# Residual block on one core: the last chunk's outer weight combinations in three operations of 1024 columns

## The chip, the cores and the metric

The kernel runs on one core of a Trainium2 chip. The metric is device time in microseconds (us), and less is better. Several runs are timed, and one further kind of record, the profile, shows a single execution instruction by instruction. The engines are named as in the profile: PE is TensorE (matrix products), DVE is VectorE, ACT is ScalarE, POOL is GpSimd, SP is SyncE, which only issues DMAs here.

## The reference

The kernel computes a residual block with a time embedding, as in diffusion models, over two images of 512 channels and 64 x 64 pixels:

```python
def gn(z, gamma, beta):              # 4 groups of 128 channels
    zr = z.reshape(B, G, (C // G) * H * W)
    mu = zr.mean(-1).reshape(B, G, 1)
    var = ((zr - mu) ** 2).mean(-1).reshape(B, G, 1)
    zn = ((zr - mu) / jnp.sqrt(var + eps)).reshape(B, C, H, W)
    return zn * gamma.reshape(1, C, 1, 1) + beta.reshape(1, C, 1, 1)
...
h = conv3(_silu(gn(x, g1, be1)), w1)      # 3x3, padding 1, 512 -> 512
emb = _silu(t_emb) @ w_emb
h = h + emb.reshape(B, C, 1, 1)
h = conv3(_silu(gn(h, g2, be2)), w2)
return x + h
```

Inputs and weights are bf16. Nearly all of the arithmetic lies in the two 3 x 3 convolutions.

## The kernel before

**Tiling.** Channels are cut into four blocks of 128 (`ct` for input, `k` for output blocks). The image is cut into two halves of 32 rows, and a convolution over one half of one image is a *chunk*. There are eight: 0 to 3 are the first convolution, 4 to 7 the second. A *unit* is one output block of one chunk, so each chunk has four units, 32 in all; the code names the unit of chunk 6 and output block 3 `u63`. Every value that is worked on lies in one large 16-bit tile in SBUF, `ar`, whose regions are given by offsets, and products land in the eight banks of `psum`.

**The convolution as a transform.** The rows of a half are transformed in groups of four, so that a 3 x 3 convolution over the rows takes six products of transformed rows (numbered 0 to 5) in place of more direct ones. 0 to 3 are the inner ones, 4 and 5 the outer ones. Along a row, a second, smaller transform ("nested") is used: the pixels are split into even and odd ones, and a product with three taps becomes four products with combined weights of 256 columns instead of three of 512. In chunks 4 to 6 the inner products are nested and the outer ones are plain; in the last chunk, 7, the outer ones are nested too. Nested products need weight combinations: of three taps w0, w1, w2 one forms w0 + w2, then (w0 + w2) + w1 and (w0 + w2) - w1.

**The last chunk.** `unit7` (line 890) is the unit of chunk 7. It calls `nest_st` (line 882), which forms the combinations of the outer weights of that unit. These weights are streamed from memory for each unit by `stream_w2` (line 664) in two loads, one for two input blocks each, into one of two sets of SBUF space (`s` is 0 or 1, by turns; `st_off` gives the place). `nest_st` forms the sums for two input blocks in three additions of 512 columns, then for the other two. The difference is written over the middle tap, in place. `B_mms`, `A_mms`, `Bo_mms` and `Ao_mms` list the matmuls of the nested products: `B` and `A` are the inner ones, `Bo` and `Ao` the outer ones. The steps of a unit are, in this order: four inner `B` steps, four inner `A` steps, two `Bo` steps and two `Ao` steps, each with eight matmuls of 256 columns. ACT copies the results from `psum` into `ar` with a scale (names `b`, `m`, `o4`, `o5`). Pairs of banks are used in turn, so a step of a unit waits until the pair's earlier result has been copied. DVE then adds: `S` (sum and difference of the nested halves), `A` (the halves added together), `s` and `d` (sum and difference of the product pairs), then the scalings by 8, 2 and 4 on the engines that `CFG["s"]` names for the chunk, `y` (the inner product sums into the result rows `ys`) and two `O` additions, which add the outer products `OS` and `OA`. A DMA on POOL's queue adds the finished unit to the output in memory, where the block's input x has been copied before. The result rows have two buffers, `YS[0]` and `YS[1]`, by turns.

The very last unit ends in `last_y` (line 1110), which works in smaller pieces and stores with three plain DMAs on SP's queue.

**What sets the order.** The kernel writes no engine's order by hand. `Plan.op` records every operation with the space it reads and writes, and an assumed cost; `Plan._run` is a list scheduler over these, which takes on each engine the ready operation of the best priority; `Plan.solve` makes the priorities in three rounds, changes them by the tables `NUDGE` and `ORDER`, and fixes the order; `Plan.emit` then writes the instructions in this order. PE's products form one chain, so their order is the order of the program. A plain DMA is paced: `emit` adds a wait for a matmul that the plan has shortly before the DMA's own place. Where an instruction stands in its engine's queue is so an outcome of the plan; on the chip the engines run in order, and wait for each other by semaphores.

All DVE additions have line 423 in the profile, all DVE scalings line 427, all ACT operations line 446, all DMAs line 459, nearly all matmuls line 474.

Of the kernel before, what the change touches and what calls it, by code (L numbers as in the profile page):

```python
# [10 lines left out]
ACT = mybir.ActivationFunctionType  # L11
ALU = mybir.AluOpType
# [9 lines left out]
class Op:  # L22
# [3 lines left out]
NUDGE = {  # L26
    ('a10', 'DMA'): -6.1,
    ('emb', 'DMA'): -4.9,
    ('k01', 'DVE'): 3.6,
    ('k10', 'DVE'): -17.9,  # L30
    ('ld_ur02', 'DMA'): -31,
    ('ld_ur11', 'DMA'): -12.6,
    ('ld_ur12', 'DMA'): 4.6,
    ('ld_ur13', 'DMA'): -26.7,
    ('ld_ur21', 'DMA'): -3.1,
    ('ld_ur23', 'DMA'): -69.1,
    ('ld_ur3', 'DMA'): -62.2,
    ('rob10', 'DVE'): -6,
    ('row11', 'DVE'): 19.2,
    ('silu00', 'ACT'): -8.7,  # L40
    ('silu11', 'ACT'): -0.4,
    ('st01', 'DVE'): 24.1,
    ('st02', 'ACT'): 36.2,
    ('st02', 'PE'): 26.8,
    ('st03', 'ACT'): 61.3,
    ('st10', 'ACT'): -3.4,
    ('st11', 'ACT'): -24.7,
    ('u004', 'DVE'): 81.3,
    ('u00d', 'DVE'): -4.5,
    ('u00y', 'DVE'): -1.5,  # L50
    ('u01m1', 'ACT'): -14.6,
    ('w1_00', 'DMA'): 12.8,
    ('w1_01', 'DMA'): -14.6,
    ('w1_03', 'ACT'): 45.4,
    ('w1_13', 'DVE'): 35.8,
    ('w1_20', 'DVE'): 27.3,
    ('w1_22', 'ACT'): 48.7,
    ('w1_22', 'DVE'): 67.4,
    ('w1_23', 'DVE'): 187.4,
    ('w1_31', 'ACT'): 16.7,  # L60
    ('w1_33', 'ACT'): 79.1,
}


ORDER = (2, (
    (204379228, 255, 30, 1),
    (234843898, 319, 120, 1),
    (211139775, 268, 30, 3),
    (669684967, 433, 15, 3),
    (1006773657, 341, 15, 3),  # L70
    (788794351, 91, 15, 3),
    (40166790, 349, 60, 1),
    (920935792, 232, 15, 1),
    (410399867, 107, 60, 0.3),
    (420875362, 192, 15, 1),
    (385567171, 251, 30, 3),
    (279912161, 95, 30, 0.3),
    (315890846, 329, 120, 1),
    (696499368, 218, 60, 1),
    (272137600, 194, 15, 0.3),  # L80
    (605732795, 129, 30, 1),
    (29479506, 139, 15, 1),
    (973994246, 204, 15, 1),
    (488781037, 250, 30, 1),
    (34394231, 99, 30, 0.3),
    (655024064, 49, 30, 0.3),
    (144588941, 58, 60, 0.3),
    (252865214, 352, 15, 1),
    (1046031975, 342, 30, 1),
    (242005847, 138, 15, 1),  # L90
    (974414065, 143, 15, 1),
    (73604465, 212, 30, 3),
    (659385421, 129, 15, 1),
    (738286652, 264, 120, 3),
    (573361134, 368, 15, 1),
))


class Plan:
# [118 lines left out]
    def solve(self, rounds=3):  # L218
        ops = self.ops
# [5 lines left out]
        pris, best = [], None  # L225
        for k in range(rounds):
            pris.append(pri)
            st, span = self._run(pri, False)
            if k + 1 == rounds:
                break  # L230
            bt, bspan = self._run([-(s + o.cost) for s, o in zip(st, ops)], True)
            pri = [-(b + o.cost) for b, o in zip(bt, ops)]
        k, moves = ORDER
        pri = np.array(pris[k]) - np.array([NUDGE.get((o.name, o.eng), 0.0) for o in ops])
        st = np.array(self._run(pri.tolist(), False)[0])
        for seed, t0, w, sg in moves:
            pri = pri + np.where((st >= t0) & (st < t0 + w), np.random.default_rng(seed).normal(size=n) * sg, 0.0)
        best = self._run(pri.tolist(), False)
        self.span = best[1]
        for o, s in zip(ops, best[0]):  # L240
            o.start = s
        return best

    PACE = 0.8
# [1202 lines left out]
```

## Time and profile before

| | us |
|---|---|
| median of 4 runs | 459.6 |
| the runs | 456.84, 458.66, 460.55, 462.36 |
| the profiled execution, its own time | 462.36 |
| its span, from first to last instruction | 460.4 |
| busy: PE, DVE, ACT, POOL | 444.6, 432.7, 391.9, 66.6 |

The profile's lines are read as follows. A group line has the source line, the engine, the operation, what it writes and reads, shapes and count; then the busy time in us and the mean of one in ns; then how long the engine stood idle just before such instructions and what ended most of that idle time. A timeline line has start, duration, engine and operation, a count of merged instructions, and in brackets the idle time before them and who ended it. A line of the stretches has for each engine the busy time and, in brackets, the number of instructions. A matmul's own duration is longer than its distance to the next one, since matmuls are pipelined.

### The profile page before, as it was taken

What the parts mean: (1) busy time and instruction counts of PE and PEld (TensorE: products, weight loads), DVE (VectorE), ACT (ScalarE), POOL (GpSimd) and SP (SyncE); (2) the same over time, 40 slices, a digit from 0 to 9 for tenths busy, and PEclk for the clock granted to TensorE, in tenths of its full rate; (3) what the DMA queues carried; (4) which work ended last, traced back from release to release, by engine and by line L of the source; (5) the groups of instructions that cost most, each with busy time, mean ns of one, the idle gap of its engine ahead of it and who ended that gap; (6) DMA issues with size and microseconds to landing.
All of it is one profiled execution on the core that took longest, in us unless ns stands there. A gap on an engine that the chain in (4) does not pass through costs nothing. (4 is left out here: it accounts for less than half of the span.)

```text
span 460.4 us, 8314 instructions
## 1 busy us (share of the span) xinstructions
PE 444.6 (97%) x2866; PEld 279.0 (61%) x2866; DVE 432.7 (94%) x865; ACT 391.9 (85%) x620; POOL 66.6 (14%) x94
## 2 busy tenths in 40 slices
PE   7897999999999999999999999999999999999993
PEld 4553444455555555555555577776666777778883
DVE  3887999999998999989999999998899999999997
ACT  5849999999999998699996699849997999567663
POOL 2140002112121122210210001121111111011211
PEclk9898999999999999999999999999999999999998
DMA  8962469979979687988898566857985864462844
GB/s 321 399 207 80 131 179 258 247 201 261 279 238 239 180 250 203 246 276 281 232 324 306 180 246 198 206 148 151 213 199 115 200 182 107 111 162 39 184 103 93
DMA packets 45977, 94.10 MB, mean 204 GB/s; under 512 B 7024, under 2 KB 18160, under 8 KB 45936
## 3 DMA queue, kind: packets, MB, share of 16 engines
q1 hardware_dynamic: 35712, 77.60, 50.6%
q0 software_dynamic: 9936, 15.98, 22.9%
q8 instruction: 22, 0.36, 0.3%
q14 instruction: 19, 0.16, 0.1%
q10 hardware_dynamic: 288, 0.01, 0.0%
HBM read 62.25 MB, written 31.32 MB: 203 GB/s over the span
## 5 line engine op out<-in xcount | busy, mean ns | idle before, releaser
L474 PE MATMUL psum<-ar 128*128 128x256 f16 (+2 forms) x2739 | 429.9, 320 | 4.7 <-DVE ar L423 3.7
L423 DVE TENSOR_TENSOR ar<-ar 128x1024 f16<-128x1024 f16 (+6 forms) x692 | 403.5, 647 | 12.0 <-ACT ar L446 7.5
L474 PEld LDWEIGHTS <-ar 128*128 128x128 f16 (+1 forms) x2775 | 268.3, 98 | 165.0 <-issue 8.8
L446 ACT ACTIVATE ar<-ar 128x512 f16<-128x512 f16 (+6 forms) x204 | 181.0, 920 | 20.3 <-DVE ar L423 16.5
L446 ACT ACTIVATE ar<-psum 128x512 f16<-128x512 f32 (+3 forms) x227 | 156.9, 721 | 30.8 <-PE psum L474 15.3
L446 ACT ACTIVATE ar<-ar,fs 128x2112 f16<-128x2112 f16 (+3 forms) x36 | 70.5, 1966 | 1.1 <-DMA ar<-h_scr 0.9
L459 POOL DMA_DIRECT2D ar<-ar x30 | 30.5, 1040 | 163.2 <-DVE ar L423 84.1
L459 POOL DMA_DIRECT2D out_dram<-ar x15 | 18.2, 1210 | 94.6 <-DVE ar L423 94.6
L427 DVE TENSOR_SCALAR ar<-ar 128x512 f16<-128x512 f16 (+4 forms) x74 | 24.8, 347 | 2.7 <-ACT ar L446 2.7
L446 ACT ACTIVATION_READ_ACCUMULATOR ar<-psum 128x1 f32 x96 | 21.2, 221 | 0.0
L463 POOL MEMSET ar<- 128x65 f16 (+6 forms) x30 | 5.4, 226 | 80.8 <-DVE ar L423 35.8
L446 ACT ACTIVATION_READ_ACCUMULATOR ar<-ar 128x1 f32 x50 | 10.2, 203 | 0.0
L559 POOL TENSOR_TENSOR fs<-fs 128x1 f32<-128x1 f32 x4 | 6.8, 1692 | 22.3 <-DVE fs L555 22.3
L474 PE MATMUL psum<-ar,ones_bf 128*128 128x260 bf16 x40 | 6.8, 333 | 2.0 <-DMA ar<-in_x_dram 1.1
L1188 DVE BATCH_NORM_STATS2 fs<-ar 128x6 f32<-128x416 bf16 x15 | 8.0, 580 | 0.0
L567 POOL TENSOR_TENSOR fs<-fs 128x4 f32<-128x4 f32 x3 | 4.0, 1348 | 21.4 <-DVE fs L555 21.4
L474 PEld LDWEIGHTS <-ones_bf 128*128 128x128 bf16 x40 | 4.7, 119 | 4.1 <-issue 2.8
L474 PEld LDWEIGHTS psum<-fs,ones_neg 128*128 128x128 f32 x42 | 5.9, 196 | 1.8 <-DVE fs L1192 1.0
L446 ACT ACTIVATE fs<-fs 128x1 f32<-128x1 f32 x4 | 1.5, 384 | 6.1 <-POOL fs L560 6.1
L474 PE MATMUL psum<-fs,ones_neg 128*128 128x1 f32 (+3 forms) x42 | 5.4, 242 | 0.9 <-DVE fs L1192 0.9
L545 DVE TENSOR_SCALAR fs<-psum 128x2 f32<-128x2 f32 x4 | 0.6, 158 | 5.1 <-PE psum L474 4.6
L489 PE MATMUL psum<-ones_bf 128*128 128x512 bf16 x9 | 4.0, 631 | 1.1 <-DVE ones_bf L480 1.1
(46 smaller groups left out, 19.7 us busy)
## 6 DMA issues: line engine op xcount, KB each, us to landing
ar<-in_w_dram SPq DMA_DIRECT2D x32, 384.0 KB, 4.9
ar<-in_x_dram SPq DMA_DIRECT2D x16, 552.5 KB, 4.9
h_scr<-ar SPq DMA_DIRECT2D x16, 520.0 KB, 3.5
ar<-h_scr SPq DMA_DIRECT2D x16, 520.0 KB, 4.2
out_dram<-in_x_dram SPq DMA_DIRECT2D x30, 260.0 KB, 4.1
ar<-ar POOLq DMA_DIRECT2D x30, 260.0 KB, 4.7
out_dram<-ar POOLq DMA_DIRECT2D x15, 520.0 KB, 6.2
u_scr<-ar SPq DMA_DIRECT2D x16, 384.0 KB, 4.0
```

The lines of the kernel that those rows point to most:

```text
L423: return pl.op("DVE", 0.075 + 0.000521 * out.n, lambda: nc.vector.tensor_tensor(out=out.ap, in0=a.ap, in1=b.ap, op=op), regs(a, b), regs(o ...
L427: pl.op("DVE", cost or 0.075 + 0.00026 * out.n, lambda: nc.vector.tensor_scalar(out=out.ap, in0=a.ap, scalar1=s, scalar2=None, op0=ALU.mul ...
L446: lambda: nc.scalar.activation(out=out.ap, in_=a.ap, func=func, scale=sc, **kw), regs(*rr), regs(*ww), name)
L459: lambda: eng.dma_start(out=out, in_=in_, **kw), regs(*r), regs(*w), name, lat=lat or (3.2 if sw else None), after=after, sw=sw)
L463: pl.op("POOL" if eng == "gpsimd" else "DVE", 0.08 + 0.0005 * out.n, lambda: e.memset(out.ap, v), (), regs(out), name)
L474: ins = nc.tensor.matmul(out.ap, lhsT=lhsT.ap, rhs=rhs.ap, start=st, stop=sp, skip_group_check=True)
L489: nc.tensor.matmul(psum[:, 0:512], lhsT=ones_bf[:], rhs=wr, start=True, stop=True, skip_group_check=True)
L545: pl.op("DVE", 0.16, lambda: V.tensor_scalar(out=F(tot, 2 * n).ap, in0=ps.ap, scalar1=YF / HW, scalar2=None, op0=ALU.mult), regs(ps), regs ...
L559: nc.gpsimd.tensor_tensor(out=N.ap, in0=N.ap, in1=F(NEGH, n).ap, op=ALU.pow)
L567: pl.op("POOL", 0.85 if n == 1 else 1.9, lambda: nc.gpsimd.tensor_tensor(out=F(rs, n).ap, in0=N.ap, in1=F(NEGH, n).ap, op=ALU.pow), regs(N ...
L1188: pl.op("DVE", 0.07 + 0.00104 * d.n, lambda d=d, i=i: V.bn_stats(out=F(BNS + 6 * i, 6).ap, in_=d.ap), regs(d), regs(F(BNS + 6 * i, 6)), name)
```

## The change

`nest_st` forms the combinations for all four input blocks in three additions of 1024 columns, and the difference goes to new space, at 10496 columns behind the start of the region of chunk 6's transformed rows, rather than over the middle tap. `Bo_mms` reads it there. That space belongs to the third of four input blocks of chunk 6, which the inner products of chunk 6's last unit still read. For the three units of chunk 7 ahead of the last one, the scalings by 8 and 4 go from DVE to ACT, and the second `O` addition becomes an accumulating DMA on POOL's queue (`o7`). The planner's assumed cost of a 512-column matmul is a little higher. Its rounds and the two tables are replaced by one table of priorities, a number for each operation, which is used directly.

```diff
+PRI = (
+    3887, 4299, 4467, 4151, 4299, 4149, 4525, 4510, 4472, 4466, 4462, 4459, 4452, 4446, 4443, 4455, 4465, 4445, 4440, 4436, 4433, 4426, 4422, 4409,
...
+)
...
-        k, moves = ORDER
-        pri = np.array(pris[k]) - np.array([NUDGE.get((o.name, o.eng), 0.0) for o in ops])
-        st = np.array(self._run(pri.tolist(), False)[0])
-        for seed, t0, w, sg in moves:
-            pri = pri + np.where((st >= t0) & (st < t0 + w), np.random.default_rng(seed).normal(size=n) * sg, 0.0)
-        best = self._run(pri.tolist(), False)
+        assert len(PRI) == n
+        best = self._run([-p / 10.0 for p in PRI], False)
...

-    's': ((D_, D_, D_), (D_, D_, D_), (D_, A_, A_), (D_, D_, D_), (A_, A_, A_), (A_, A_, A_), (A_, A_, A_), (D_, A_, D_)),
+    's': ((D_, D_, D_), (D_, D_, D_), (D_, A_, A_), (D_, D_, D_), (A_, A_, A_), (A_, A_, A_), (A_, A_, A_), (A_, A_, A_)),
+    'o7': (0, 1),
...
-            cost += {512: 0.2195, 256: 0.109, 384: 0.166}.get(rhs.n, max(0.0715, rhs.n / 2330.0)) * warm
+            cost += {512: 0.2202, 256: 0.109, 384: 0.166}.get(rhs.n, max(0.0715, rhs.n / 2330.0)) * warm
...
-            w = (A(LV + 4160 + ucnt[0] % 2 * 1024 + ct * 256 + (s - 4) * 128, [[1, 128]]) if q == 0 else
-                 A(st_off(ucnt[0] % 2, ct) + (s - 4) * 384 + 128, [[1, 128]]))
+            w = A(LV + (10496 if q else 4160) + ucnt[0] % 2 * 1024 + ct * 256 + (s - 4) * 128, [[1, 128]])
...
     def nest_st(s, nm):
-        for h in range(2):
-            g = lambda kx, dt=BF16: A(st_off(s, 2 * h) + kx * 128, [[384, 4], [1, 128]], dt)
-            t = A(LV + 3136 + h * 512, [[128, 4], [1, 128]])
-            tt(t, g(0), g(2), ALU.add, nm)
-            tt(A(LV + 4160 + s * 1024 + h * 512, [[128, 4], [1, 128]]), t, g(1), ALU.add, nm)
-            tt(g(1, None), t, g(1), ALU.subtract, nm)
+        g = lambda kx: A(st_off(s, 0) + kx * 128, [[UM, 2], [384, 4], [1, 128]], BF16)
+        n = lambda o: A(LV + o, [[512, 2], [128, 4], [1, 128]])
+        tt(n(3136), g(0), g(2), ALU.add, nm)
+        tt(n(4160 + s * 1024), n(3136), g(1), ALU.add, nm)
+        tt(n(10496 + s * 1024), n(3136), g(1), ALU.subtract, nm)
...
-        tt(yo, yo, A(OS, [[PL, 2], [1, PL]]), AD, nm + "O")
-        tt(yo, yo, A(OA, [[PL, 2], [1, PL]]), AD, nm + "O")
+        for i, o in enumerate((OS, OA)):
+            oo = A(o, [[PL, 2], [1, PL]])
+            if CFG["o7"][i]:
+                dma(yo.ap, oo.ap, [oo, yo], [yo], P * 4 * PL, nm + "oa", sw=True, acc=True)
+            else:
+                tt(yo, yo, oo, AD, nm + "O")
```

## The prediction

> **What bounds the kernel now.** I read the page's busy shares first, then the table of busy time by stretches, then what TensorE (PE) waited for, and then, for every place where PE stood still, the timeline of the engine it waited for.
>
> ```profile
> PE 444.6 (97%) x2866; PEld 279.0 (61%) x2866; DVE 432.7 (94%) x865; ACT 391.9 (85%) x620; POOL 66.6 (14%) x94
> ...
> 333.50:345.00 11.50, 10.59 (x73) 6.96 (x72) 11.40 (x18) 11.29 (x13) 2.22 (x3) 1.00 0.81 200
> ...
> 414.00:425.50 11.50, 11.39 (x105) 10.04 (x104) 11.50 (x25) 7.71 (x12) 1.22 (x1) 1.00 0.26 36
> 425.50:437.00 11.50, 11.50 (x108) 10.30 (x107) 11.50 (x25) 7.89 (x11) 2.41 (x2) 1.00 0.90 179
> 437.00:448.50 11.50, 11.50 (x108) 10.30 (x106) 11.50 (x24) 7.30 (x11) 1.20 (x1) 1.00 0.51 115
> 448.50:460.00 11.50, 4.71 (x44) 3.96 (x41) 8.79 (x19) 5.01 (x8) 1.20 (x1) 0.86 0.46 93
> ```
>
> In the stretches the columns are PE, PEld, DVE, ACT and POOL busy, PE's granted clock, DMA share and GB/s. The last chunk (from about 410 us) shows two engines full: PE, with 108 matmuls in each 11.5 us, and VectorE (DVE), 11.50 of 11.50. Only one of them can set the end. The timeline decides:
>
> ```profile
> 39.43 8.86 PE L474 MATMUL psum<-ar 128*128 128x512 f16 x32 [2.75 <-DVE ar L423]
> ...
> 337.22 9.05 PE L474 MATMUL psum<-ar 128*128 128x512 f16 x57 [0.91 <-ACT ar L446]
> ...
> 435.80 17.41 PE L474 MATMUL psum<-ar 128*128 128x256 f16 x158
> ...
> 421.61 0.42 PEld L474 LDWEIGHTS <-ar 128*128 128x128 f16 x4 [0.28 <-issue]
> ...
> 444.37 12.44 DVE L423 TENSOR_TENSOR ar<-ar 128x512 f16<-128x512 bf16 x26
> 456.72 0.68 DVE L1142 TENSOR_TENSOR ar<-ar,psum 128x512 bf16<-128x512 f16 x1
> ```
>
> From 39.43 us on PE has two holes, 0.91 us before 337.22 and 0.28 us at 421.6; everything else follows back to back. 158 matmuls of 256 columns take 17.41 us; less the pipelined excess of the last (0.27 - 0.11) that is 109 ns from start to start, and in these stretches it doesn't vary. So PE's last matmul, at 453.2, is 39.4 us of opening, then a stream that no cheaper DVE instruction shortens, plus 1.2 us of holes. Behind it stand 4.2 us of DVE (to 457.4) and 3.0 us of last store (to 460.4). DVE is full, but it is the follower: it works off results that PE delivers. A saving on DVE can reach the time only through the 1.2 us of holes or the 4.2 us tail.
>
> **The change part by part.** Durations are rows of the groups by shape; two DVE instructions in a row overlap by about 0.08 us (425.37 and 425.57 are the starts of a 0.28 us scaling and its successor), so a 512-column addition (0.42) costs 0.34 in the queue, one of 1024 or 1040 columns (0.69) 0.61, a 512-column scaling (0.28) 0.20; on ScalarE (ACT) a 512-column scaling (0.63) costs 0.53.
>
> ```profile
> L423 DVE TENSOR_TENSOR ar<-ar 128x1024 f16<-128x1024 f16 x226 | 151.3, 690 | 4.5 <-ACT ar L446 4.1
> ...
> L423 DVE TENSOR_TENSOR ar<-ar 128x512 f16<-128x512 f16 x86 | 34.1, 421 | 1.3 <-DMA ar<-ar 1.3
> ...
> L446 ACT ACTIVATE ar<-ar 128x512 f16<-128x512 f16 x50 | 30.3, 631 | 8.5 <-DVE ar L423 7.8 <-DVE fs L569 0.3
> ...
> ar<-ar POOLq DMA_DIRECT2D x30, 260.0 KB, 4.7
> out_dram<-ar POOLq DMA_DIRECT2D x15, 520.0 KB, 6.2
> ```
>
> - Weight combinations: 24 additions of 512 columns become 12 of 1024: 24 x 0.34 - 12 x 0.61 = 0.8 us less DVE. Their pattern (two blocks of four pieces of 128) is not in the trace; the 1024-column row, which holds similar pieces, gives 0.61, and two separate 512 ones would be 0.68. Below 0.61 nothing is expected, since the element rate is the same.
> - Scalings by 8 and 4 of three units: 6 x 0.20 = 1.2 us less DVE, 6 x 0.53 = 3.2 us more ACT, which had 3 to 4 us free in each stretch above.
> - One outer addition of three units becomes an accumulating DMA on POOL's queue: 3 x 0.61 = 1.8 us less DVE, three issues of 1.0 us on a queue that is 14% busy.
> - Sum: 3.9 us less DVE in the last chunk, and none of it is on PE. After the last matmul the same instructions remain. In the present tail the second product pair leaves ACT at 450.8 (timeline), DVE takes it at 451.0, and 6.4 us of DVE and ACT work follow. With 3.9 us saved, DVE waits for that evacuation; the row addition that the new order puts in front of it makes it up to 0.2 us late, one addition fewer (0.61) is left behind it, and the chain of scalings by 2, 4 and 8 (3 x 0.6 on ACT, each in front of a DVE addition) fills that gap. Last matmul to DVE's end: 4.2 us before, 4.2 to 4.3 after. Tail: +0.1, between -0.6 (the whole addition comes off) and +0.3.
>
> The new table of priorities (PRI) also reorders the rest. Put side by side, the two programs have the same PE order but for one swap, the same opening but for one DVE swap of 0.2 us that falls into a wait for PE (0.6 us at 26 us), and single swaps up to 320 us. Two places matter:
>
> - The hole at 337: PE waits for an ACT evacuation with a full ACT queue ahead of it. The set ahead is unchanged; but the scaling by 8 now stands before two instructions (1.1 us) that used to precede it, and reaches its DVE input about 0.2 us too early. 0.91 becomes 1.1; bounds 0.5 and 1.4.
> - The hole at 421.6: PE waits for a bank whose evacuation (419.6 to 421.6 on ACT) waited 1.88 us for DVE to finish chunk 6's last output addition. Ahead of that addition DVE now has one 1024-column operation of chunk 7's row transform more (+0.6) and the smaller weight set (3 x 0.61 - 6 x 0.34 = -0.2): +0.4 us on a DVE without gaps since 372, plus the 0.2 from the first hole. The stall restarts PE at 422.2 instead of 421.6, whatever happened to it before.
>
> Path: +0.6 from the second hole (the first is contained in it), +0.1 tail, less rounding: about **+0.6 us**. The profiled execution took 462.4 us (span 460.4 and 2.0 around it), so it would take 463.0. It is the slowest of the four runs; the same shift on their median 459.6 gives **460.2 us**. About 1% (4.6 us) is what a measurement of this kernel can tell from no change.
>
> What is added as a wait, and its cover: a unit's store now follows addition, accumulating DMA (4.7 us) and store (6.2 us) where it followed two additions. The buffer of the first unit is written again at 445.0, and its first outer addition ends at 430.2: 430.2 + 10.9 = 441.1, 3.9 us spare. The second: 440.4 + 10.9 = 451.3 against 454.2, 2.9 spare. The third store: 447.9 + 10.9 = 458.8, against 459.0 for the last store's landing: just hidden. If it is not, each microsecond of lateness is a microsecond of time.
>
> [...] The trace has GpSimd issuing its DMAs in 1.0 us (accumulating) and 1.2 us (stores) beside a full DVE, but of two equal small GpSimd operations on data the second lasted until DVE ran dry:
>
> ```profile
> 24.95 1.00 POOL L559 TENSOR_TENSOR fs<-fs 128x1 f32<-128x1 f32 x1 [6.77 <-DVE fs L555]
> ...
> 30.22 4.47 POOL L559 TENSOR_TENSOR fs<-fs 128x1 f32<-128x1 f32 x1 [4.00 <-DVE fs L555]
> ```
>
> [...] By the rows above the additions cost nothing, and I take the rows.
>
> **Rivals.**
> - *DVE's relief reaches the time* (0.15). For it: DVE has no idle time from 372 to 456, and both holes lead back to it or to ACT. If the new order removes both holes (-1.2) and the tail loses its addition (-0.6): -1.8, 457.8. Against: the second hole stands before the saving starts.
> - *A late weight set turns into a PE hole: slower* (0.17). A combination over both halves needs both loads. The second load for the third unit is paced behind a matmul that stands about 31 matmuls (3.4 us) further on; now it is issued at 423.8 and lands 4.7 later. In the new kernel: issue 427.6, landing 432.4, first use in DVE's queue near 433.6, 1.2 us spare. Behind that instruction wait the difference, the two scalings now on ACT, and behind those the evacuation of the outer banks, now last in ACT's queue, which PE needs about 0.6 us later. So beyond 1.8 us of lateness each microsecond is lost on PE; together with the store at the end I price it at +1 to +3, 461 to 463. A chance of 0.08 is kept within it for over 1%, if two links go together.
> - *The opening changes* (0.06). PE's wait of 2.75 before 39.43 comes from the 4.47 us operation. If the swap frees it, up to 2.75 goes: 456.9. Against: the DVE instructions around it are the same.
>
> **How the numbers follow.** Forecast 0.62 (own range 459.2 to 461.2), relief 0.15, late weights 0.17, opening 0.06. The range takes in the relief case with a margin of 0.5 for the spread of medians, and the late-weight case to +2.6: 457.3 to 462.8. That leaves out most of the opening case and the upper half of the late-weight case, 0.15. Over 1% faster needs the opening and the holes together: 0.04. Over 1% slower: 0.08. Within: 0.88.
>
> **What the next profile would show.** Right: PE's last matmul near 453.8, holes near 337 and 422, DVE with gaps in the last 35 us and busy some 3.9 us less, ACT some 3 us more, the last DVE operation 4.2 to 4.3 us after the last matmul. Wrong: PE holes between 422 and 453, a DVE wait for a load near 434, accumulations landing later than 7 us, an opening that ends elsewhere than 39.4, or a tail under 3.7 us.

## The result, and the profile after

The changed kernel takes 462.45 us (median of 39 runs, 460.57 to 472.56). The kernel before, run beside it on the same chips, takes 458.42 (60 runs, 456.39 to 463.49). The ratio is 1.008, with a 95% interval of 1.0061 to 1.0098: some 3.7 us slower (2.8 to 4.5). The ratio leaves out runs that lie more than 1.5% above the fastest of the same kernel. The forecast was +0.6 us.

The two profiled executions say the opposite. That of before took 462.36 us (span 460.4), that of after 460.6 (span 458.7). The difference is an opening that is long in one execution and short in another, in both kernels, as the experiments show. So the profiles are compared below by the length of one stretch and not by the span.

The first line of the page of after, the busy time of each engine:

```profile
PE 442.1 (96%) x2866; PEld 277.6 (61%) x2866; DVE 429.7 (94%) x844; ACT 395.9 (86%) x626; POOL 68.3 (15%) x97
```

DVE has 21 instructions fewer (12 + 6 + 3, as the change has it) and 3.0 us less to do; ACT has 4.0 us more. The timeline of PE from the restart after the hole that stood at 337 in before to the last matmul, first in before, then in after:

```profile
337.22 115.99 PE L474 MATMUL psum<-ar 128*128 128x512 f16 x912 [0.91 <-ACT ar L446]
```

```profile
332.76 84.28 PE L507 MATMUL psum<-ar 128*128 128x512 f16 x624 [0.24 <-ACT ar L479]
417.65 15.88 PE L507 MATMUL psum<-ar 128*128 128x256 f16 x144 [0.61 <-ACT ar L479]
433.96 10.64 PE L507 MATMUL psum<-ar 128*128 128x256 f16 x96 [0.43 <-ACT ar L479]
444.90 5.40 PE L507 MATMUL psum<-ar 128*128 128x256 f16 x48 [0.30 <-ACT ar L479]
```

Before had one nearly unbroken line of 115.99 us here. After has three breaks, two of them (0.43 and 0.30) inside the last chunk. The last DVE operation now ends 5.15 us after the last matmul (455.45 against 450.30); it was 4.19.

The chain that ended last tells what the new breaks are made of. Its lines in after are start, duration, and who:

```profile
428.63 5.58 DMA ar<-in_w_dram
...
434.33 1.31 DVE ar L456 x2
...
436.20 5.52 DMA ar<-ar
...
442.31 3.46 ACT ar L479 x5
...
445.80 1.30 DVE ar L456 x2
```

The chain begins with a weight load. Then comes the DVE operation that waited for it, then the accumulating DMA of the second unit, then ACT, which waited for that DMA, then the tail. Before, no load and no DMA stood in this place.

The stretches of after (columns as before: PE, PEld, DVE, ACT, POOL, clock, DMA share, GB/s) answer to those shown of before:

```profile
414.00:425.50 11.50, 10.89 (x100) 9.59 (x99) 10.52 (x18) 7.96 (x12) 2.42 (x2) 1.00 0.62 111
425.50:437.00 11.50, 11.06 (x102) 9.76 (x100) 10.43 (x17) 9.06 (x14) 3.21 (x3) 1.00 0.73 158
437.00:448.50 11.50, 11.20 (x103) 9.87 (x102) 8.54 (x14) 8.24 (x13) 2.81 (x3) 1.00 0.73 113
```

DVE, full in before (11.50 of 11.50), has 1 to 3 us free in each. PE has less to show than before, not more: the relief of DVE went into waits.

**Where the 3.5 us are.** Laid over each other at the same places of the program, the two profiled executions differ like this:

| stretch | before | after | difference |
|---|---|---|---|
| first DVE operation of the second image's statistics (near 272 / 267) to the restart of PE at 337.22 / 332.76 | 65.25 | 66.02 | +0.77 |
| restart to the end of the second hole (421.61 / 417.65) | 84.39 | 84.89 | +0.50 |
| from there to the last matmul's end (453.21 / 450.30) | 31.60 | 32.65 | +1.05 |
| last matmul's end to the end of the span | 7.19 | 8.40 | +1.21 |
| sum | | | +3.53 |

What lies ahead of the first row varies by some 5 us from one execution to the next, and no run measures its mean. The sum, 3.5, is near the 3.7 us of the timed runs, but it is of one pair of profiles. The last three rows are together the time from the restart to the end of the span: 123.18 us in before, 125.94 in after. This is the measure that the experiments are read by, because it doesn't contain the opening.

### The profile page after: what moved, and what is told of

Its sections match the earlier page's. It is cut to its first block, busy times and chain, and to the rows that moved or that the text cites. A ratio compares the mean times of both kernels' runs of the same rounds, so it can differ in the third digit from the quotient of the medians.

```text
span 458.7 us, 8299 instructions
## 1 busy us (share of the span) xinstructions
PE 442.1 (96%) x2866; PEld 277.6 (61%) x2866; DVE 429.7 (94%) x844; ACT 395.9 (86%) x626; POOL 68.3 (15%) x97
## 5 line engine op out<-in xcount | busy, mean ns | idle before, releaser
L479 ACT ACTIVATE ar<-ar 128x512 f16<-128x512 f16 (+6 forms) x210 | 184.2, 910 | 22.1 <-DVE ar L456 19.2
L492 POOL DMA_DIRECT2D ar<-ar x33 | 34.1, 1051 | 161.8 <-DVE ar L456 94.0
L460 DVE TENSOR_SCALAR ar<-ar 128x512 f16<-128x512 f16 (+4 forms) x68 | 23.0, 353 | 0.0
L496 POOL MEMSET ar<- 128x65 f16 (+6 forms) x30 | 6.4, 256 | 83.3 <-DVE ar L456 29.8
L507 PE MATMUL psum<-ar,ones_bf 128*128 128x260 bf16 x40 | 5.6, 283 | 2.7 <-DMA ar<-in_x_dram 2.1
L600 POOL TENSOR_TENSOR fs<-fs 128x4 f32<-128x4 f32 x3 | 5.9, 1958 | 14.8 <-DVE fs L588 14.7
L592 POOL TENSOR_TENSOR fs<-fs 128x1 f32<-128x1 f32 x4 | 2.6, 660 | 21.8 <-DVE fs L588 21.8
```

The source lines that it names most:

```text
L460: pl.op("DVE", cost or 0.075 + 0.00026 * out.n, lambda: nc.vector.tensor_scalar(out=out.ap, in0=a.ap, scalar1=s, scalar2=None, op0=ALU.mul ...
L479: lambda: nc.scalar.activation(out=out.ap, in_=a.ap, func=func, scale=sc, **kw), regs(*rr), regs(*ww), name)
L492: lambda: eng.dma_start(out=out, in_=in_, **kw), regs(*r), regs(*w), name, lat=lat or (3.2 if sw else None), after=after, sw=sw)
L496: pl.op("POOL" if eng == "gpsimd" else "DVE", 0.08 + 0.0005 * out.n, lambda: e.memset(out.ap, v), (), regs(out), name)
L507: ins = nc.tensor.matmul(out.ap, lhsT=lhsT.ap, rhs=rhs.ap, start=st, stop=sp, skip_group_check=True)
L592: nc.gpsimd.tensor_tensor(out=N.ap, in0=N.ap, in1=F(NEGH, n).ap, op=ALU.pow)
```

## The experiments

The theory from the two traces: the wide combination needs both halves of a unit's weights at once, so the second load of the last unit is late, and the accumulating DMA holds the single buffer `OA` until it has landed. The rivals: only the one or only the other; the order of the rest that the new table brought; the opening. Except in `b0`, `b1` and `h3`, the order of the changed kernel is held by its planned start times (`START`) in place of the priorities, so that only the edit moves. The measure "to the end" is restart of PE to end of span, with the hole ahead of the restart beside it; "tail" is the last matmul's end to DVE's last end.

| kernel | ratio to before (95%) | hole ahead | to the end | tail |
|---|---|---|---|---|
| before | | 0.91 | 123.18 | 4.19 |
| after | 1.008 (1.0061 to 1.0098) | 0.24 | 125.94 | 5.15 |
| f1_no_acc | 1.0103 (1.0043 to 1.0163) | 2.64 | 126.71 | 5.51 |
| f4_two_oa | 1.0095 (1.0059 to 1.0131) | 1.11 | 126.39 | 5.16 |
| f5_halves | 1.0102 (1.003 to 1.0175) | 2.63 | 125.53 | 5.16 |
| b1_nest_old_order | 1.005 (1.0023 to 1.0076) | 1.37 | 123.96 | 5.00 |
| b0_before | one time, 458.96 us | 1.03 | 123.26 | 4.19 |
| g1_early_load | 1.0063 (1.0019 to 1.0107) | 1.75 | 123.66 | 4.12 |
| g2_both | 1.0173 (1.0114 to 1.0233) | 1.19 | 127.43 | 4.20 |
| g3_no_acc_early | 1.011 (1.0051 to 1.017) | 1.62 | 124.48 | 4.95 |
| h1_late_use | one time, 468.46 us | 2.63 | 129.19 | 5.15 |
| h2_early_swap | 1.0071 (1.0029 to 1.0112) | | | |
| h3_before_open | 0.9992 (0.9958 to 1.0026) | 0.34 | 123.24 | 4.19 |
| h4_best | 1.0087 (1.0052 to 1.0122) | 2.05 | 125.35 | 4.79 |

**f1_no_acc: both outer additions on DVE.**

```diff
-    'o7': (0, 1),
+    'o7': (0, 0),
```

> The changed kernel with every engine's order held, but the second outer addition of the three units is again a VectorE addition, at the place in the order where the accumulating DMA was issued (VectorE 3 x 0.61 us more). Held-buffer theory (the accumulating DMA reads the only buffer of the outer plane sums until it lands, so ScalarE's next evacuation into it waits): ScalarE's waits of 1.18 us before 433.07 and 1.38 us before 441.57 go, with them the PE holes of 0.43 us before 433.96 and 0.30 us before 444.90, and the tail goes from 5.15 us back to about 4.2: 1.5 to 1.7 us off the time, some 459 in a profile with the short opening. Late-load theory (the combination over both halves waits for the second half of the third unit's weights): the hole before 433.96 stays at 0.4 us or grows, as VectorE has more to do, and at most 0.7 us goes. Order theory (what was lost comes from the order alone): nothing changes by more than 0.3 us.

Measured: no better (126.71). The accumulating DMA is gone and so is ACT's wait for it, but another DMA falls onto the weight load. The waits of f1 from 420 to 455 us (engine and line, whom it waited for: total, times, longest), and below them the landing times of the weight loads in that window:

```profile
DVE ar L456 <- DMA ar<-in_w_dram: 2.2, 1, 2.2
```

```profile
DMA to landing us min/median/max: 3.2/5.4/7.1
```

```profile
447.96 5.40 PE L507 MATMUL psum<-ar 128*128 128x256 f16 x48 [1.52 <-ACT ar L479]
```

The first unit's 520 KB store no longer waits for an accumulating DMA: it is issued at 430.45, 95.3 us after the restart, where after issues it 100.8 us behind its own (433.58), and so it runs beside the load. The load takes 7.1 us to land, DVE waits 2.2 us for it, and PE stands still for 1.52 us ahead of its last 48 matmuls (the third fence, PE's timeline). So the accumulating DMA alone is not the cause; taking it away puts the same loss on the load.

**f4_two_oa: two buffers for the second outer product, by turns.**

```diff
-        BO, OS, OA = LV, LV + 1024, LV + 2064
+        BO, OS, OA = LV, LV + 1024, LV + (12608 if u % 2 else 2064)
```

> The changed kernel with every engine's order held and the accumulating DMAs kept; the outer plane sums alternate between two buffers, so that an evacuation no longer waits for the DMA that reads the other one. Held-buffer theory: ScalarE's two waits (1.18 and 1.38 us) go, the holes before 433.96 and 444.90 go or halve, the tail is 4.2 to 4.5 us: 1.2 to 1.7 us off, at least as much as without the DMAs. Late-load theory: VectorE's wait of 0.94 us at 434.08 and the hole of 0.43 us before 433.96 stay; 0.5 us or less goes. If the DMA hurts in another way (its issue, its traffic beside the weight loads), this run stays with the changed kernel and the one without the DMAs does not.

Measured: no better (126.39). The waits of f4 in the same window:

```profile
ACT ar L479 <- DVE ar L456: 8.1, 6, 3.5
...
DVE ar L456 <- DMA ar<-in_w_dram: 2.4, 2, 2.1
```

ACT, which waits for DVE here, waits for no DMA any more, so the buffer was the cause of that wait. But the load lands later still, DVE waits 2.1 us for it, and PE has a hole of 0.80 at 444.86. The tail is that of after.

**f5_halves: the combinations in two halves again, in the new space.**

```diff
+        for h in range(2):
+            g = lambda kx: A(st_off(s, 2 * h) + kx * 128, [[384, 4], [1, 128]], BF16)
+            n = lambda o: A(LV + o + h * 512, [[128, 4], [1, 128]])
```

> The changed kernel with every engine's order held, but each weight combination is again made in two halves of 512 columns (24 operations in place of 12, into the same new space; 0.8 us more VectorE over the four units), the first half first, so that only the second half waits for the second load. Late-load theory: VectorE's wait of 0.94 us at 434.08 goes, filled by the first half, and with it the hole of 0.43 us before 433.96 and about 0.4 us of the tail: 0.5 to 0.9 us off. Held-buffer theory: the hole of 0.43 us is ScalarE's, which waited for the buffer, so it stays, and the tail stays at about 5 us; nothing changes by more than 0.3 us, or 0.2 us is lost to the additional operations.

Measured: 125.53, and the tail of after. The waits of f5 in this window:

```profile
DVE ar L456 <- ACT ar L479: 3.8, 4, 2.2
ACT ar L479 <- DMA ar<-ar: 2.7, 3, 1.1
```

Now DVE waits for ACT and for no load, and ACT still waits for the accumulating DMA. f1, f4 and f5 together: there are two late things, each covered by the other, and the one that is left costs what the two did. Single removals could not show that; it took one that removes what both come from. f5 also says little on the width: in the order of after the two halves follow each other, so the second half's turn, 101.5 us after the restart, comes only as late as the load's landing there.

**b1_nest_old_order: the wide combinations alone**, with the priorities, scalings and additions of before.

```diff
+    's': (..., (D_, A_, D_)),
+    'o7': (0, 0),
...
+        best = self._run([-p / 1000.0 for p in PRI], False)    # priorities of the kernel before
```

> The kernel before with its own priorities, and only the weight combinations changed: 3 operations of 1024 columns, the difference into the new space; scalings and outer additions as before. Held-buffer theory: no accumulating DMA from the outer buffer, so no new wait; within 0.5 us of the kernel before, VectorE 0.8 us less busy. Late-load theory: a VectorE wait for the weight load near 438 and a PE hole of 0.4 us or more behind it. Order theory: within 0.5 us of the kernel before.

Measured: the ratio is 1.005, and the profile shows 123.96 to the end. PE's timeline:

```profile
333.94 115.95 PE L507 MATMUL psum<-ar 128*128 128x512 f16 x912 [1.37 <-DMA ar<-in_w_dram]
```

No hole in the last chunk, no wait for a load of it: in this order the wide combination of the last unit is taken 102.9 us after the restart, and its second load landed 0.5 us before. What is worse is the tail, 5.00: two other additions, 1.3 us, came to stand ahead of the second product pair's. The profile accounts for 0.8 us; the timed difference is 2.3 us (1.0 to 3.5), so part of it is not explained.

**b0_before: the kernel before once more**, unchanged, for the part that differs by chance.

> The kernel before, unchanged, for a second profile. If the 4.47 us of the GpSimd operation at 30.2 us in its first profile was one outcome of two, this one shows about 0.7 to 1.0 us there, no PE hole before 39.4, an own time of 457 to 459 us, and the same 123.2 us (within 0.3) from TensorE's restart near 333-337 to the end. If the operation is always that slow in this kernel and fast in the changed one, 4.5 us again and 461 to 463.

Measured: everything from 65 us ahead of the restart on is as in before (123.26 to the end, the tail 4.19). The opening is not. Here are GpSimd's timelines of before (shown with the prediction: 4.47 us) and of b0; it is the same instruction of the same program:

```profile
30.59 0.68 POOL L559 TENSOR_TENSOR fs<-fs 128x1 f32<-128x1 f32 x1 [3.99 <-DVE fs L555]
```

4.47 us in one execution, 0.68 in another. Behind the long form PE stands still for 2.75 us (the prediction shows it at 39.43), and then its granted clock is low for some 3.4 us: 0.59 and 0.55 in the two stretches from 40 to 44 us of before, where after, with the short form, shows 1.00 from 28 to 46 us. The mean clock of the execution is 0.989 in before and 0.993 in b0. Between PE's 181st and 261st matmul before takes 18.95 us and b0 14.54. That is why the profile of after (14.54 too) looked faster than that of before; b0's span, 456.9, is shorter than after's 458.7.

**g1_early_load: the last unit's weights into a third space, loaded 17.5 us earlier in the plan.**

```diff
-        return UREG[2 * s + ct // 2] + 8192 + (ct % 2) * 768
+        return (LV + 12544 + ct * 768) if s == 2 else UREG[2 * s + ct // 2] + 8192 + (ct % 2) * 768
...
-                stream_w2(ucnt[0] % 2, k)
+                stream_w2(2 if ucnt[0] == 31 else ucnt[0] % 2, k)
```

> The changed kernel with every engine's order held; only the last unit's outer weights go into a third set of their own and are loaded some 20 us earlier, so that their combination waits for no load. The outer buffer is still held by the accumulating DMA. Measure: the time from TensorE's restart after its hole near 333-337 us to the end of the span (before 123.2 us, changed kernel 125.9 us, changed without the DMAs 126.7, with two outer buffers 126.4). Two-causes theory (held buffer and late load each make the same VectorE and ScalarE work late, and the one hides the other): 125.3 to 126.2, VectorE's wait of 0.94 us before 434.08 goes, ScalarE's wait for the buffer before 441.57 stays. Late-load theory alone: 124.6 or less.

Measured: 123.66 to the end, 2.28 us less than after, and the tail is 4.12. PE's timeline of g1:

```profile
337.74 84.28 PE L507 MATMUL psum<-ar 128*128 128x512 f16 x624 [1.75 <-ACT ar L479]
422.63 31.60 PE L507 MATMUL psum<-ar 128*128 128x256 f16 x288 [0.61 <-ACT ar L479]
```

The waits and the DMA issues of g1 from 420 to 455 us, with the accumulating DMA's median time to landing at the end of the last line:

```profile
DVE ar L456 <- ACT ar L479: 2.7, 4, 1.1
```

```profile
ar<-ar POOLq DMA_DIRECT2D x3, 260.0 KB, 3.8
```

And the same kind of line of after:

```profile
ar<-in_w_dram SPq DMA_DIRECT2D x3, 384.0 KB, 5.6
ar<-ar POOLq DMA_DIRECT2D x3, 260.0 KB, 5.5
```

288 matmuls run without a break. DVE waits for no load and ACT for no DMA, although there is still one buffer `OA`. The first unit's accumulating DMA, issued 94.3 us after the restart in both, lands in 3.78 us where it took 6.22 with the last unit's two loads issued just behind it; the second one, which in after ran beside the delayed store of the first unit, in 4.33 rather than 5.52. So the last unit's loads, in that place, were the root of both. The third unit's load, which g1 leaves where it was, lands only 0.2 us ahead of its use. The timed ratio, 1.0063, does not separate g1 from after: the intervals overlap widely, and g1's ten runs lie between 459.0 and 466.4. A gain of 2.3 us (a ratio of some 1.003) lies within g1's interval, and so does no gain. The recovered 2.3 us are shown by the profile, not by the times.

**g2_both: g1, and a second buffer for the outer product.**

```diff
-        BO, OS, OA = LV, LV + 1024, LV + 2064
+        BO, OS, OA = LV, LV + 1024, (BT0 if u % 2 else LV + 2064)
```

> As the run before it, and the outer plane sums alternate between two buffers: neither the late load nor the held buffer is left, all else as in the changed kernel. Two-causes theory: the PE holes of 0.43 and 0.30 us (near 434 and 445) go, the tail (last matmul to VectorE's end) falls from 5.15 us to 4.2-4.5: 124.0 to 124.8 us from the restart to the end, that is 1.2 to 1.8 us less than the changed kernel; the hole of 0.6 us near 418 stays, as it comes from the order. Order theory (the new order, not these waits, holds VectorE and ScalarE back): 125.4 or more.

Measured: 127.43 to the end, with PE holes of 1.62 and 1.19 us at 419 and 421 us. The second buffer was put into space that the last chunk's own outer products still read, so this kernel changes that part of the computation and puts new waits in front of it. It says nothing on the question.

**g3_no_acc_early: g1, and both outer additions on DVE.**

```diff
-    'o7': (0, 1),
+    'o7': (0, 0),
```

> The changed kernel with every engine's order held, without the accumulating DMAs (VectorE adds, 3 x 0.61 us more) and with the early load. Two-causes theory: neither cause is left, so VectorE's wait of 2.17 us for the load and the PE hole of 1.52 us behind it go, and of the 126.7 us from the restart to the end that the run without the DMAs took 124.2 to 125.0 are left. If the DMAs were worth their 1.8 us of VectorE, this run is behind the one with two buffers by up to that; if VectorE only follows TensorE here, the two agree within 0.3 us. Order theory: 126 or more.

Measured: 124.48 to the end, the tail 4.95. PE's timeline of g3:

```profile
334.02 84.28 PE L507 MATMUL psum<-ar 128*128 128x512 f16 x624 [1.62 <-ACT ar L479]
418.92 31.60 PE L507 MATMUL psum<-ar 128*128 128x256 f16 x288 [0.61 <-ACT ar L479]
```

PE's stream is the same to the hundredth. With DVE doing the additions again the tail is 0.8 us longer than in g1. So in these two profiles the accumulating DMAs are a gain of 0.8 us in the tail, once the load is early; the times do not separate the two.

**h1_late_use: the last unit's combinations later in DVE's queue**, so that they wait for the load at the end of what DVE can do.

```diff
-    427.06, 429.50, 431.26    # planned starts of the three combinations of u73
+    429.00, 432.00, 433.00
```

> The changed kernel with one move in VectorE's order and nothing else: the three combinations of the last unit stand later in VectorE's queue (the first behind the unit's outer addition and two row transforms, 1.9 us later), so that VectorE no longer stands in front of the weight load; load and accumulating DMA keep their places and still run into each other. Measure: TensorE's restart after its hole near 333-337 us to the end of the span (before 123.2, changed 125.9, with the early load 123.7). If VectorE's place in the queue is what costs: 123.5 to 124.3, no VectorE wait for the load, no PE hole near 445, tail 4.1 to 4.5 us. If the collision itself costs (accumulating DMA landing some 6 us after its issue, ScalarE waiting 1.2 us for its buffer before 433): the hole of 0.43 us near 434 stays and 124.6 to 125.6.

Measured, one run: worse, 129.19 to the end (1.65 us of it a low clock, 0.58 and 0.57 in the two stretches from 338 to 342: the 624 matmuls after the restart take 85.93 us, and 84.28 in after, f1, f4, f5, g1 and g3). The waits and PE's timeline of h1:

```profile
DVE ar L456 <- DMA ar<-in_w_dram: 1.7, 1, 1.7
```

```profile
441.82 10.64 PE L507 MATMUL psum<-ar 128*128 128x256 f16 x96 [2.53 <-ACT ar L479]
```

Here it was the load of the third unit, not the last one, that came late: the loads took 6.4 us at the median, the accumulating DMAs 7.0. It is inconclusive on the place in the queue, but it shows that the third unit's load, too, can fail in an execution.

**h2_early_swap: g1, with one row addition of 1040 columns of chunk 7 put back behind chunk 6's last output addition.**

```diff
-    407.41    # planned start of the row addition rob73
+    408.90    # behind u63y
```

> The run with the early load, and two neighbours in VectorE's order changed back to the order of the kernel before: chunk 6's last row combination before a 1040-column row transform of chunk 7 (0.6 us), not behind it. My step on the second hole: the PE hole of 0.61 us near 418-422 goes back to 0.0 to 0.15 us, nothing else moves: 123.0 to 123.3 us from the restart to the end, against 123.7. Rival: ScalarE's own queue or the smaller weight set sets that hole; 0.5 us or more stays and the stretch is 123.6 or more.

Measured: 1.0071. Its one profile is of an execution of 467.8 us, where the fastest of this kernel took 459.9, with a low clock right after the restart (0.71 and 0.50 in the two stretches from 340 to 344 us), so its times are not read here. The second hole is not in it, and the third unit's load came late again: DVE waited 1.0 us for it. The same edit is in h4.

**h3_before_open: before, and DVE waits for GpSimd in the opening**, so that the two do not run side by side there.

```diff
+            if o is nx:
+                tc.add_manual_dep(ins.ins, self.pw, sync, reason="port")
```

> The kernel before with one wait added in the opening: the VectorE operation that follows the clamp of the fourth channel group's statistics waits for the GpSimd power operation (0.7 us when it is not held up, 4.47 us in the first profile of before). Theory: the long one is an outcome of chance in which back-to-back VectorE operations keep GpSimd out; with the wait it can't happen, PE's hole of 2.75 us near 39 never shows, the times lose their upper group (460 to 463.5) and the median is 457.0 to 458.2, at a cost of up to 0.9 us in the executions that were fast. Rival: the wait holds the whole opening up, 1 us or more in every execution; median 458.5 to 459.5.

Measured: 0.9992 (0.9958 to 1.0026), no difference. The expectation, no times above 460 and a median of 457.0 to 458.2, is not met: the median is 459.08, and four of twelve runs took 460.0 or more. GpSimd's and PE's timelines of h3, with PE's line of b0 at the same place last:

```profile
29.35 0.55 POOL L565 TENSOR_TENSOR fs<-fs 128x1 f32<-128x1 f32 x1 [3.99 <-DVE fs L561]
```

```profile
32.27 5.01 PE L480 MATMUL psum<-ar 128*128 128x512 f16 x15 [1.71 <-DVE ar L429]
...
333.56 116.02 PE L480 MATMUL psum<-ar 128*128 128x512 f16 x912 [0.34 <-DMA ar<-in_w_dram]
```

```profile
32.75 3.46 PE L474 MATMUL psum<-ar 128*128 128x512 f16 x15 [0.95 <-DVE ar L423]
```

The GpSimd operation is short (0.55), and from the restart on all is as in before. But the added wait lengthens PE's pause from 0.95 to 1.71 us, and the 15 matmuls behind it take 5.01 us against 3.46; the mean granted clock is 0.987 against 0.993 in b0. Between PE's 181st and 261st matmul h3 takes 16.72 us, 2.2 more than b0; the long form costs 4.4 there (18.95). Five of the twelve profiles without this wait have the long form, so an estimate of the saving is 5/12 of 4.4, 1.8 us: the wait costs about what it saves.

**h4_best: g1, with the edits of h2 and h3.**

```diff
+    START of g1, with rob73 behind u63y
...
+                tc.add_manual_dep(ins.ins, self.pw, sync, reason="port")
```

> The changed kernel with the early load, the two neighbours swapped back, and the wait of the opening: all that the runs found. Theory: from the restart to the end as the kernel before (123.0 to 123.4 us), and no long GpSimd operation in the opening: median 457.0 to 458.5, at or a little below the kernel before. Rival: what the change costs lies elsewhere too, ahead of the restart (the new order up to 330 us); then 459 or more.

Measured: 1.0087 (1.0052 to 1.0122), no better than after. PE's timeline has no break after the restart:

```profile
335.95 117.43 PE L513 MATMUL psum<-ar 128*128 128x512 f16 x912 [2.05 <-ACT ar L485]
```

The second hole (0.6 us in g1) is gone, but the tail went from 4.12 to 4.79: DVE's lateness, which had shown as a hole of PE, came back at the end. The third unit's load was late by 0.33 us here. And this execution lost some 1.6 us to a low clock right after the restart (0.57 from 336 to 340 us; 117.43 us of stream against 84.28 + 31.60 in g1; the last section shows it). Without that it would be some 123.7 to the end, the same as g1. h4 also carries h3's wait (16.71 us between those two matmuls of the opening), so its times are no test of the other two edits. No version tried is faster than before.

## Why the prediction was right or wrong

**The bound, and that DVE's saving is not on the path: right.** DVE lost 3.0 us of work (forecast 3.9), ACT gained 4.0 (forecast 3.2), and nothing of it shortened the time. The combinations of 1024 columns take 0.69 us each, as taken from the row of before.

**The second hole, "+0.4 us on a DVE without gaps": right.** It measures +0.50 after the restart in the table of stretches, and putting back the one row addition that the step named (h4) removes the hole. That the gain then goes to the tail was not foreseen.

**The first hole, "The set ahead is unchanged": 0.77 us where 0.2 was forecast.** The hole's own length (0.24 to 2.64) is no measure, since it holds what the stream ahead of it lost or gained. But from the second image's statistics to the restart, all four profiles with the old order take 65.25 to 65.28 us, all nine with the new order (without h2) 66.02 to 66.06. The difference lies in one of the "single swaps up to 320 us" that I put aside as nothing. GpSimd's timeline at the power operation of these statistics, first of before, then of after:

```profile
306.82 1.49 POOL L567 TENSOR_TENSOR fs<-fs 128x4 f32<-128x4 f32 x1 [8.44 <-DVE fs L555]
308.68 1.25 POOL L459 DMA_DIRECT2D out_dram<-ar  x1 [0.37 <-DVE ar L423]
```

```profile
302.06 1.21 POOL L492 DMA_DIRECT2D out_dram<-ar  x1 [8.92 <-DVE ar L456]
303.36 3.03 POOL L600 TENSOR_TENSOR fs<-fs 128x4 f32<-128x4 f32 x1
```

And DVE's timeline of after, at the operation that needs the result:

```profile
306.42 0.16 DVE L602 TENSOR_TENSOR fs<-fs 128x4 f32<-128x4 f32 x1 [0.94 <-POOL fs L600]
```

The operation takes 1.49 us in the old order (before, b0, b1, h3) and 3.03 or 3.04 in the new one (after, f1, f4, f5, g1, g3, h1, h4), and DVE stands still for 0.94 us. It also starts 1.76 us later, counted from the first operation of these statistics, because the DVE scaling that it reads now stands behind two more additions. With the short form it would still have been in time: DVE's turn at its result comes 38.74 us after that first operation, and a start at 36.61 plus 1.49 is 38.10. Two things differ around it: the order of the DVE additions beside it, and the store's issue, which comes after it in the old order and directly ahead of it in the new one. Which of the two makes it slow, no run here tells; that it is the order, and not chance, is shown by these profiles, in which neither number differs by more than 0.04 us within an order. That this delay is the 0.77 us is read from the waits; no run undoes it alone.

**The tail, "+0.1, between -0.6 and +0.3": wrong.** It measures +0.96 to DVE's end and +1.21 to the end of the span. The step went wrong ahead of the tail: DVE came to it late, because of the load below. With the load early (g1) the tail is 4.12, 0.07 shorter than before and within the step's bounds.

**The late weight set: the right rival, the wrong unit, and too low a chance.** The trace begins as the rival does (load, DVE's wait), and the price of +1 to +3 us holds the 2.28 us that g1 measures. The rest of the way is another: it ran through the second unit's accumulating DMA and the buffer `OA`, not through the difference. PE's first hole, before 433.96, even stands ahead of DVE's wait: it comes from the first unit's accumulating DMA, which landed at 433.29, 6.22 us after its issue.

For the third unit, which the rival was worked out for, the issue and the use came within 0.4 us of the forecast, 90.5 and 96.6 us after the restart. But the sum took 4.7 us for the landing, where before shows 5.3 (423.76 to 429.05), and in after it took 6.0: of the 1.2 us spare, 0.1 was left. This load came late by 0.30 us in f4, 0.33 in h4 and 1.66 in h1.

The last unit was not looked at, and in after it is the worse one: its second load is issued at 428.63 and lands at 434.21, while its combination's turn in DVE's queue comes at 433.39. In before this load was issued at 434.68, landed at 439.77, and was first needed at 444.37, when DVE came to the second half: 4.6 us to spare. Counted from the restart, that need moved forward by 6.5 us (107.15 to 100.63) and the load only by 1.6 (97.46 to 95.87). b1, the wide combination in the order of before, needs it at 102.93, so some 4.2 of the 6.5 us come from the width and 2.3 from the new order; the width alone left 0.5 us. The chance of 0.17 stood on one unit alone.

**"just hidden": the accumulating DMA's cover was counted on the wrong buffer.** The prediction followed the buffer that it adds to, `YS`, and found 2.9 to 3.9 us spare. The buffer that it reads, `OA`, is single, and ACT writes it again one unit later. This wait of after, from 420 to 455 us, is what was missing:

```profile
ACT ar L479 <- DMA ar<-ar: 3.2, 3, 1.4
```

It costs nothing in g1, where these DMAs land in 3.8 to 4.3 us, and shows in after, where the first two take 6.2 and 5.5. The cover on `YS` itself held: the third unit's store landed at 455.81, ahead of the last store's 457.40.

**GpSimd beside a full DVE.** The rows that the prediction took are those of the DMA issues, 1.0 and 1.2 us. In after the three accumulating DMAs took 1.21 us each to issue, the stores beside them 1.20, and in g1 they land after 3.8 us at the median, beside a DVE that stood still for 2.7 of 35 us. For GpSimd's operations on data the runs show different durations, 0.68 or 4.47 us in the opening and 1.49 or 3.03 near 303, and what makes one long was not shown. A busy DVE alone does not: in before, at 306.82, the operation took 1.49 us beside a DVE that ran additions without a break, and in after, at 29.39, 0.68 beside one that was busy for 1.98 and 2.00 us of the two stretches from 28 to 32, where before has 4.47 at 30.22.

**The numbers.** The forecast of +0.6 us was right in the second hole alone, and three terms were missing or too small: 0.2 taken for 0.77 at the first stretch (and then contained in the second), nothing for 1.05 of holes in the last chunk, 0.1 for 1.21 behind the last matmul. The time of 462.45 lies at the upper end of the range (457.3 to 462.8), which reached so far for the late-weight rival, and a ratio of 1.008 is within the 1% that had most of the chance. In part that is luck: the range stood on 459.6, the median of four runs, and allowed +3.2 on it; sixty runs give 458.42, and the shift of some 3.7 us is more than that. The signs that were named as showing it wrong (holes of PE between 422 and 453, a DVE wait for a load near 434, an opening that ends elsewhere) are those that came. That the wait stands at 434.33 is chance: the sign meant the third unit's load, on the times of before, and what came is the last unit's, in a profile whose restart is 4.5 us earlier.

**Open.** Which neighbour makes the power operation at 303 us slow, and whether undoing it gives back the 0.77; the 1.5 us of b1 that its profile doesn't show; why g1's recovered 2.3 us are not visible in its times. For the last one the record has a hint: the pause ahead of the restart is 0.34 to 1.37 us in the four profiles with the old order, and up to 2.64 with the new one, where a low clock followed it in three of ten (0.62 in h1, 0.50 to 0.71 in h2, 0.57 in h4). g1's runs have a mean clock of 0.9888 against 0.9899 of after, by which, as an estimate, 0.5 us of 460 are lost.

## What to carry to other kernels

When operations are merged into wider ones, write down for every unit when each input that the wide operation now needs is issued, lands, and is taken at its place in the engine's queue; the saving in instructions (3.0 us of DVE here) bought nothing while DVE stood still for a load (0.94 us ahead of 434.33), and it was the tightest unit that counted. The DMA that took over an addition held its source as well as its target until it landed (ACT waited 3.2 us for the source in after), and landed later beside two loads (6.22 us after its issue, against 3.78 without them), so both buffers need a margin by the slow landing. Where two late transfers cover each other, removing either can show nothing (f1 126.71 and f4 126.39 us to the end, after 125.94); look for the one edit upstream that removes both.

## What the runs showed of the hardware

**The granted clock fell after a pause of 2.05 us, and not after every one of 2.6.** In h4 PE stood still for 2.05 us ahead of 335.95. The stretches around it (PE, PEld, DVE, ACT, POOL, granted clock, DMA share, GB/s):

```profile
333.50:336.00 2.50, 0.45 (x5) 0.25 (x4) 2.36 (x4) 2.50 (x5) 0.15 (x1) 1.00 0.89 340
336.00:340.00 4.00, 4.00 (x11) 1.42 (x11) 4.00 (x7) 4.00 (x4) 1.21 (x1) 0.57 0.69 174
340.00:342.00 2.00, 2.00 (x19) 1.66 (x18) 2.00 (x4) 1.47 (x3) 0.90 (x1) 1.00 1.04 172
```

The granted clock fell to 0.57 for 4 us, in which 11 matmuls ran where g1 has 25 in its first 4 us, and some 1.6 us were lost. In h1 it fell after 2.63 us (0.62 from 337.3 to 341.5), in h2 after 2.64 (0.71 and 0.50 in the two stretches from 340 to 344); in f1 (2.64) and f5 (2.63), after the same pause in the same place, it stayed at 1.00. So the length of the pause alone does not tell: a low clock followed 2.05 us in h4, and none followed 2.64 in f1. In the opening of before it fell after the pause of 2.75 us (0.59 and 0.55 from 40 to 44 us). The five profiles with that pause (before, g1, g2, h1, h2) have a mean granted clock of 0.983 to 0.989 (in h1 and h2 the drop after the restart is in it), the seven with the short operation and no added wait 0.990 to 0.993. Behind the pause of 1.71 us in the opening of h3 and h4, 15 and 18 matmuls took 5.01 and 5.66 us; behind one of 0.95 us, 15 took 3.46 in b0 and 18 took 4.12 in after, where the clock stayed at 1.00.

**Landing times differed with what ran beside.** The first unit's accumulating DMA of 260 KB from SBUF to SBUF landed 5.8 to 8.3 us after its issue where the last unit's two loads were issued within 1.6 us behind it (f5 5.8, after 6.2, f4 and h1 8.3), and after 3.8 to 4.6 us where they were not (g1 3.8, h4 3.9, h2 4.6). The third unit's two weight loads of 384 KB landed after 5.5 and 5.3 us in before and after 5.4 and 6.0 in after. In f1 the slowest load took 7.1 us, with a 520 KB store issued 0.6 us before it; the three stores from 415 to 440 us took 7.2 us at the median there, and 6.2 in after.

**One GpSimd operation, two durations.** The same small operation of the same program took 0.68 us in b0 and 4.47 in before; with the low clock behind it that is 4.4 us of PE's time (18.95 against 14.54). So a single profile of this kernel says nothing on 3 to 5 us of the opening, whichever kernel it is of.
